# Row groups of a Fourier stage interleaved on the partitions, start-up transfers re-ordered, nine zero products ahead of the first

## The chip, the core and the metric

The program runs on one core of one Trainium2 chip. The metric is the device time of one execution in microseconds (us), lower is better. TensorE (PE), VectorE (DVE), ScalarE (ACT) and GpSimd (POOL) each run their own instruction stream in order and meet at semaphores; SyncE (SP) only issues DMAs here, in order.

## What is computed

A global filter in the frequency domain over 8 sequences of 2496 tokens with 256 channels, then a mixture of 8 experts in which each token goes to one.

```python
X = np.fft.rfft(x, axis=1)                       # x: (8, 2496, 256)
Yr = Xr @ w_r - Xi @ w_i + b_r
Yi = Xr @ w_i + Xi @ w_r + b_i
Yr, Yi = soft_shrink(Yr, 0.01), soft_shrink(Yi, 0.01)
y = np.fft.irfft(Yr + 1j * Yi, n=2496, axis=1)   # becomes x of the experts, 19968 tokens
e_idx = argmax(x @ w_gate + modality_bias[modality_id], axis=1)
out[mask_e] = gate * (relu(x[mask_e] @ w1[e]) @ w2[e])
```

## The kernel before

The Fourier transform of 2496 points is split into 39 times 64. Per sequence (a "batch", b = 0 to 7) there are these stages. **s1**: the length-39 transform as a matrix product. `x[b]` is seen as 39 rows (n1) of 64 (n2) by 256 channels; three groups of n2 (starting at 0, 22 and 42, the tuple `GB`) stand at once on 117 partitions, group g on partitions 39 g to 39 g + 38. One load covers 4 or 8 values of n2 and is three DMAs, one per group (`s1_load`, L228). The 22 values of n2 per group are worked off in 11 chunks of two: `s1_split` writes the high part (L242) and the rest (L243) of a chunk, `s1_chunk` makes three products with the block matrix `c_f` (L261 to L263), ACT copies the 120 resulting rows out of PSUM (L266), and the copies are stored to a scratch tensor in DRAM, `scr`, again with three DMAs, one per group of 40 rows (L277). For batch 0 the stores go out after the chunks 3, 7, 9 and 10. **s2**: for a pair of the 20 frequencies k1, `a_load` reads 128 rows back from `scr` (L286) and `s2_pair` multiplies them with a table `c_m` (L295). A load of batch 0 can start only when all its stores have landed, since each pair needs every n2. **mix** (L332) multiplies with the complex weights `wmix`, **is2** (L356) with a table `c_q`, then **pivot** (L372) and **is1** (L384) give the result, `Route` computes gate and place of each token and scatters the rows to their experts. `SplitWeights` prepares the expert weights meanwhile. From about 610 us on, `Experts` runs the two expert products (L819, L849) to the end.

PE's order is written out by hand in `build`. Batch 0 goes first: 11 chunks of s1, then chunks 0 to 5 of batch 1 (the loop with `ahead1 = 6`) with s2 of the pairs 0 and 1 and the first mix between them, then a loop over pairs p in which s2, mix and is2 of batch 0 run beside the rest of batch 1's chunks; later batches repeat the pattern. The order in which SP issues DMAs is set by the program order and by `tc.issue_after`, which places DMAs behind a given one in SP's queue. Loads for batch 0 and batch 1's first five pieces have buffers of their own. POOL issues no plain DMA; it scatters rows by indirect DMAs (L547, L862) and computes some differences (L994, L799).

Of the kernel before, what the change touches and what calls it, by code (L numbers as in the profile page):

```python
# [23 lines left out]
D = 256  # L24
# [30 lines left out]
def shape_constants(nb):  # L55
# [14 lines left out]
    for k1 in range(K1):  # L70
# [12 lines left out]
    blk_f = np.zeros((P1, PK))
    blk_g = np.zeros((PK, P1))
    for g in range(3):
        blk_f[g * N1:(g + 1) * N1, g * 2 * K1:(g + 1) * 2 * K1] = fwd
# [41 lines left out]
class Attn:  # L128
# [24 lines left out]
    def consts_first(self):  # L153

        nc, I, cp = self.nc, self.I, self.cp
        self.m = cp.tile([128, K1 * 128], F32, name="c_m")
        self.q = cp.tile([128, K1 * 128], F32, name="c_q")
        self.f = cp.tile([P1, 2, 128], F32R, name="c_f")
        st = self.w1.tile([128, 2, 256], F32, tag="u", name="st_f")[:P1].rearrange("p a b -> p (a b)")[:, :256]
        nc.sync.dma_start(st, I["c_f"])  # L160
        nc.vector.tensor_copy(self.f, st.rearrange("p (h k) -> p h k", h=2))

        self.w = cp.tile([128, 2, 2, 2, 256], F32R, name="wmix")

        self.bias = cp.tile([128, 256], F32, name="bias")

        self.nlam = cp.tile([128, 16], F32, name="nlam")[:, :1]
        nc.vector.memset(self.nlam, -LAM)

    def table_load(self, t, k):  # L170

        o = slice(k * 512, (k + 1) * 512)
        return self.nc.sync.dma_start((self.m if t == "m" else self.q)[:, o], self.I["c_" + t][:, o])

    def consts_mix(self):
        nc, I, cp = self.nc, self.I, self.cp
        st = []
        for i, nm in enumerate(("w_r", "w_i")):
            st.append(self.ww.tile([128, 520], F32, tag="wr", name=f"st_w{i}")[:, :512].rearrange("p (c d) -> p c d", c=2))
            nc.sync.dma_start(st[i], I[nm].rearrange("(c p) d -> p c d", p=128))  # L180
        for i, nm in enumerate(("b_r", "b_i")):
            nc.sync.dma_start(self.bias[64 * i:64 * i + 64, :],
                              I[nm].rearrange("(o d) -> o d", o=1).to_broadcast([64, 256]))
        yield
        for i in range(2):
            nc.vector.tensor_copy(self.w[:, i, :, 0, :], st[i])
            nc.vector.tensor_sub(self.w[:, i, :, 1, :], st[i], self.w[:, i, :, 0, :])
# [20 lines left out]
            nc.vector.tensor_copy(self.pv[:, c, go:go + E], gst[:, c, :])  # L208


    def s1_load(self, b, u, end=None, eng=None):

        nc = self.nc
        eng = eng or nc.sync
        end = end or u + 1
        n = min(4 * end, J) - 4 * u
        xv = self.I["x"][b].rearrange("(a c) d -> a c d", c=N2)
        if b < 2 and u < 5:

            if u == 0:  # L220
                self.early = self.x1f[0] if b else self.w1.tile([128, 2 * N2, K1, 2], F32, tag="z", name="x_0")
                if not b:
                    self.early = self.early.rearrange("p n k r -> p (n k r)")
            xt = self.early[:P1, u * 4 * D:end * 4 * D].rearrange("p (j d) -> p j d", d=D)
        else:
            xt = self.wx.tile([P1, 4, D], F32, tag="x", name=f"x_{b}_{u}")
        for g in range(3):
            ins = eng.dma_start(xt[g * N1:(g + 1) * N1, :n, :], xv[:, GB[g] + 4 * u:GB[g] + 4 * u + n, :])  # L228
        for v in range(u, end):
            self.xt[b, v] = xt[:, 4 * (v - u):4 * (v - u) + 4, :]  # L230
        return ins

    def s1_split(self, b, c):
        nc = self.nc
        u, h = c // 2, c % 2
        for v in (u, u + 1):
            if v < 6 and (b, v) not in self.xt:
                self.s1_load(b, v)
        x = self.xt[b, u][:, 2 * h:2 * h + 2, :].rearrange("p j d -> p (j d)")
        xh = self.w6.tile([P1, 512], F32R, tag="x1h", name=f"x1h_{b}_{c}")  # L240
        xl = self.w6.tile([P1, 512], F32R, tag="x1l", name=f"x1l_{b}_{c}")
        (nc.vector.tensor_copy if b == 1 or b == 0 and c % 2 == 0 else nc.scalar.copy)(xh, x)  # L242
        nc.vector.tensor_sub(xl, x, xh)  # L243
        self.xs[b, c] = xh, xl

    def s1_chunk(self, b, c, ahead):

        nc = self.nc
        u, h = c // 2, c % 2
        xh, xl = self.xs.pop((b, c))  # L250
        if c == 0:
            self.scr[b] = self.dr.tile([2 * K1, N2, D], F32, tag="scr", name=f"scr_{b}")
        if h == 0 and b:
            self.ev = self.w3.tile([128, 4 * D], F32, tag="ev", name=f"ev_{b}_{u}")[:PK].rearrange("p (j d) -> p j d", d=D)
        if b == 0:

            self.ev = self.x1f[1][:PK, :J * D].rearrange("p (j d) -> p j d", d=D)[:, 4 * u:min(4 * u + 4, J), :]

        pool, tag = (self.rps, "r") if b == 1 or c < 2 else (self.ps, "x" if b and c < 9 else "y")
        ps = pool.tile([128, 512], F32, tag=tag, name=f"s1_{b}_{c}")  # L260
        nc.tensor.matmul(ps[:PK], self.f[:, 0, :PK], xh, start=True, stop=False)  # L261
        nc.tensor.matmul(ps[:PK], self.f[:, 1, :PK], xh, start=False, stop=False)
        nc.tensor.matmul(ps[:PK], self.f[:, 0, :PK], xl, start=False, stop=True)  # L263
        if ahead and c + ahead < 11:
            self.s1_split(b, c + ahead)
        nc.scalar.copy(self.ev[:, 2 * h:2 * h + 2, :].rearrange("p j d -> p (j d)"), ps[:PK])  # L266
        if b == 0:
# [732 lines left out]
def build(tc, I, out, nb):  # L1000
    nc = tc.nc
    with ExitStack() as outer:
        dp = outer.enter_context(tc.tile_pool(name="wsp", bufs=1, space=DRAM))
        wsp = dp.tile([E * 128, 8192], F32, name="wsp")
        with ExitStack() as ctx:
            at = Attn(tc, I, nb)
            rt = Route(outer, tc, I, at, nb)
            at.pools(ctx)
            ctx.enter_context(tc.manual_schedule(engines={ET.PE, ET.Activation, ET.DVE, ET.Pool}))
            sw = SplitWeights(tc, I, at.ww, at.wo, wsp)  # L1010
# [35 lines left out]
            for u, v in ((0, 1), (1, 3), (3, 5)):  # L1046
                at.s1_load(0, u, v)
            first = at.s1_load(0, 5)
            at.s1_split(0, 0)
            at.s1_split(0, 1)  # L1050
            mixing = at.consts_mix()
            for c in range(11):
                at.s1_chunk(0, c, 2)
                with tc.issue_after(at.stored.ins if c > 2 else first.ins):
                    if c == 3:
                        at.table_load("m", 0)
                    elif c == 7:
                        at.s1_load(1, 0)
                    elif c == 9:
                        ins = at.s1_load(1, 1, 3)  # L1060
            with tc.issue_after(at.stored.ins):
                next(mixing, None)
                for i in range(3):
                    ins = load(i)
                    if i < 2:
                        with tc.issue_after(ins.ins):
                            ins = at.s1_load(1, 3, 5) if i else at.table_load("q", 0)
            with tc.issue_after(ins.ins):
                at.table_load("m", 1)
                rt.load_ids(0)  # L1070
            ahead1 = 6 if nb > 1 else 0
            at.s1_split(1, 0)
            at.s1_split(1, 1)
            for c in range(ahead1):
                with tc.issue_after(ins.ins):
                    at.s1_chunk(1, c, 2)
                if c == 1:
                    s2(0)
                    next(mixing, None)
                    bias(0)  # L1080
                if c == 3:
                    s2(1)
                if c == 4:
                    mix(0)
# [143 lines left out]
```

## Time and profile before

| | before |
|---|---|
| median of 3 runs (lowest, highest) | 1543.92 us (1542.63, 1546.65) |
| profiled execution, its own time | 1546.72 us |
| profiled execution, span from first to last instruction | 1544.9 us |
| PE busy in the span | 1497.0 us, 97% |
| PE's idle time ahead of 50 us | 27.0 us of 47.9 us in all |

The profile is of one execution. Its page gives busy time per engine; "waits" lists who waited for whom; a "timeline" row reads start, duration, engine, line, operation, tiles, and in brackets the idle time of that engine just before and what ended it. SPq rows are DMA issues: the duration is that of issuing, not of moving the data.

### The profile page before, as it was taken

To read this page: it belongs to the slowest core of one execution; us is meant where nothing else is said; L and a number is where in the kernel's file an instruction comes from. 1 tells how busy PE (TensorE), PEld (TensorE's weight loads), DVE (VectorE), ACT (ScalarE), POOL (GpSimd) and SP (SyncE) were. 2 spreads that over 40 slices of the span, in tenths; PEclk is the share of its full clock that TensorE was granted. 3 is DMA by queue.
4 is the path that set the end of the run, shared out by engine and by line. 5 is a ranking of instruction groups with operands and counts; after the bars stand their busy time and mean duration, and the time that the engine had idled before them with its cause. 6 is when DMAs were issued, how large, how long until landed. Compare 5 with 4: busy or idle time off the path is not lost. (4 is left out here: it accounts for less than half of the span.)

```text
span 1544.9 us, 35019 instructions
## 1 busy us (share of the span) xinstructions
PE 1497.0 (97%) x12459; PEld 1465.4 (95%) x12459; DVE 710.1 (46%) x1497; ACT 660.0 (43%) x1345; POOL 512.8 (33%) x511
## 2 busy tenths in 40 slices
PE   4899999999999999999999999999999999999998
PEld 2899999999999989999999999999999998999998
DVE  3676666666666665444333333333333333333332
ACT  2466766676757554523232332332323222233232
POOL 0001444444444545325532232322322323223232
PEclk8899999999999999999999999999999999999999
DMA  7857786868686666523443324552225238626440
GB/s 196 247 179 261 222 269 212 277 212 277 205 261 190 207 196 236 172 44 84 110 91 80 118 55 151 163 157 43 52 47 155 53 68 306 197 40 205 111 151 33
DMA packets 289589, 244.44 MB, mean 158 GB/s; under 512 B 208448, under 2 KB 243852, under 8 KB 285161
## 3 DMA queue, kind: packets, MB, share of 16 engines
q1 hardware_dynamic: 270421, 200.60, 44.9%
q0 software_dynamic: 18992, 41.58, 8.2%
q8 instruction: 100, 1.64, 0.5%
q14 instruction: 76, 0.62, 0.1%
HBM read 432.70 MB, written 100.08 MB: 345 GB/s over the span
## 5 line engine op out<-in xcount | busy, mean ns | idle before, releaser
L849 PE MATMUL y<-w,hh 128*128 128x256 f32 x2496 | 434.6, 278 | 0.2 <-DMA w<-wsp 0.2
L819 PE MATMUL h<-xh,w 128*128 128x256 f32 x2496 | 403.8, 278 | 4.1 <-DMA w<-wsp 4.1
L849 PEld LDWEIGHTS y<-w,hh 128*128 128x128 f32 x2496 | 377.8, 188 | 1.0 <-ACT xh L798 0.3
L849 PE MATMUL y<-w,hl 128*128 128x256 f32 x1248 | 347.2, 278 | 0.3 <-DVE hl L822 0.2
L819 PEld LDWEIGHTS h<-xh,w 128*128 128x128 f32 x2496 | 339.9, 189 | 4.5 <-issue 3.9
L822 DVE SCALAR_TENSOR_TENSOR hl<-h,hh 128x512 fp32r<-128x512 f32 x312 | 209.4, 689 | 232.2 <-ACT hh L821 188.5
L862 POOL DMA_INDIRECT out<-o,ix x161 | 158.5, 984 | 427.0 <-ACT o L841 389.7
L819 PE MATMUL h<-xl,w 128*128 128x256 f32 x1248 | 245.5, 278 | 0.0
L821 ACT ACTIVATE hh<-h 128x512 fp32r<-128x512 f32 x312 | 178.2, 595 | 155.7 <-PE h L819 137.0
L849 PEld LDWEIGHTS y<-w,hl 128*128 128x128 f32 x1248 | 234.3, 188 | 1.3 <-DVE hl L822 0.9
L819 PEld LDWEIGHTS h<-xl,w 128*128 128x128 f32 x1248 | 189.6, 189 | 0.0
L841 ACT ACTIVATE o<-y,xt 128x256 f32<-128x256 f32 x78 | 37.0, 475 | 343.0 <-PE y L849 343.0
L839 DVE TENSOR_SCALAR o<-y,xt 128x256 f32<-128x256 f32 x78 | 37.7, 484 | 314.2 <-ACT o L841 310.1
L332 PE MATMUL mx<-wmix,Xh 128*128 128x256 f32 x1280 | 180.7, 284 | 0.9 <-ACT mx L312 0.6
L799 POOL TENSOR_TENSOR xl<-tr,xh 128x512 fp32r<-128x512 f32 x78 | 101.0, 1295 | 192.9 <-ACT xh L798 192.9
L332 PEld LDWEIGHTS mx<-wmix,Xh 128*128 128x128 f32 x1280 | 160.6, 189 | 3.1 <-ACT mx L312 2.7
L547 POOL DMA_INDIRECT xs<-x1b,si x88 | 88.0, 1000 | 85.2 <-ACT ph L377 33.4
L372 PE MATMUL pv<-pv,z 128*120 128x136 f32 x704 | 111.0, 283 | 0.5 <-ACT z L359 0.5
L547 POOL DMA_INDIRECT xs<-x,si x88 | 87.9, 998 | 71.2 <-ACT ph L377 32.4
L994 POOL TENSOR_TENSOR wl<-wr,wh 128x512 fp32r<-128x512 f32 x46 | 58.5, 1273 | 148.2 <-ACT wh L993 133.7
L378 DVE TENSOR_TENSOR pl<-pv,ph 120x264 fp32r<-120x264 f32 x176 | 75.9, 431 | 68.4 <-ACT ph L377 58.2
L372 PEld LDWEIGHTS pv<-pv,z 128*120 128x120 f32 x704 | 99.5, 186 | 6.7 <-ACT z L359 0.7
(186 smaller groups left out, 1998.4 us busy)
## 6 DMA issues: line engine op xcount, KB each, us to landing
w<-wsp SPq DMA_DIRECT2D x166, 2048.0 KB
a<-scr SPq DMA_DIRECT2D x80, 256.0 KB
xt<-xs SPq DMA_DIRECT2D x624, 32.0 KB
wr<-in_moe_w SPq DMA_DIRECT2D x64, 256.0 KB
wsp<-wh SPq DMA_DIRECT2D x64, 256.0 KB
wsp<-wl SPq DMA_DIRECT2D x64, 256.0 KB
scr<-ev SPq DMA_DIRECT2D x98, 160.0 KB
x<-in_x SPq DMA_DIRECT2D x96, 156.0 KB
```

The lines of the kernel that those rows point to most:

```text
L332: self.nc.tensor.matmul(ps[i][:, i, :], t[:, 2 * i + c, o:o + 128], self.w[:, wi, c, lo, :], start=False, stop=n == len(ops) - 1, skip_gro ...
L372: nc.tensor.matmul(ps[:PK, c * 128:c * 128 + D // 2 + E], self.z[:, o:o + 3, :, :].rearrange("p n k r -> p (n k r)"), self.pv[:, c, :], st ...
L378: nc.vector.tensor_sub(pl, ps[:PK, :GC], ph)
L547: i = self.nc.gpsimd.indirect_dma_start(out=self.xs, out_offset=bass.IndirectOffsetOnAxis(ap=si[:, k:k + 1], axis=0), in_=rows, in_offset= ...
L799: nc.gpsimd.tensor_sub(xl, tr, xh)
L819: nc.tensor.matmul(ps[:, q, :], w1[:, lo, c, f * 128:(f + 1) * 128], x[:, c, :], start=n == 0, stop=n == 5)
L821: nc.scalar.activation(hh[:, 2 * p:2 * p + 2, :], ps, AF.Relu)
L822: nc.vector.scalar_tensor_tensor(hl[:, 2 * p:2 * p + 2, :], ps, 0.0, hh[:, 2 * p:2 * p + 2, :], ALU.max, ALU.subtract)
L839: nc.vector.tensor_scalar_mul(o[:, s, :], y[s], gate)
L849: nc.tensor.matmul(y[s], lhsT, w2[:, lo, f, :], start=n == 0, stop=n == 23)
L862: ins = self.nc.gpsimd.indirect_dma_start(out=self.out, out_offset=bass.IndirectOffsetOnAxis(ap=ix, axis=0), in_=o, in_offset=None, bounds ...
L994: eng.tensor_sub(lo, raw, hi)
```

## The change

1. **Interleaving.** Group g of s1 now stands on every third partition from g on (`xt[g::3]`, `blk_f[g::3, g:PK:3]`), for loads and stores of all batches. Each group has 42 result rows in place of 40 (`R1`), two of them zero, so a chunk's products have 126 rows (`PS`) and `scr` has 42.
2. **Zero products.** DVE clears a tile `blank` first, and PE makes nine products of 128x512 with it ahead of the first real one; nothing reads them.
3. **Splitting of batch 0.** The differences of odd chunks are made by POOL in place of DVE, and the high parts of chunks 1, 5 and 9 by DVE in place of ACT.
4. **Transfers of the start-up.** On SP the stores of batch 0 follow each other with no load between them, and the loads of pairs 0 and 1 stand directly behind; the first piece of table `c_m` goes ahead of them. POOL issues the loads of pieces 0 and 1 of batch 1, the mix weights, the biases and the first piece of `c_q`, after its last difference. Pieces 2 to 5 of batch 1, the second piece of `c_m`, pairs 2 and 3 follow on SP; the ids of batch 0 are loaded later.
5. **PE's order.** Four chunks of batch 1 precede s2 of pair 0 in place of two; chunks 4 and 5 come after s2 of pair 2.

On PE, from the last chunk of batch 0 to the first mix, before (`s_b_c` is chunk c of batch b, `a_p` the load of pair p, `mx_0` the first mix):

```order
L263 MATMUL s_0_10_241<-x1l_10_226,c_f 120x512
L261 MATMUL s_1_0_280<-x1h_0_270,c_f 120x512
...
L263 MATMUL s_1_1_289<-x1l_1_275,c_f 120x512
L295 MATMUL s_0_0_301<-c_m,a_0_255 128x128 x4
L261 MATMUL s_1_2_319<-x1h_2_284,c_f 120x512
...
L263 MATMUL s_1_3_328<-x1l_3_294,c_f 120x512
L295 MATMUL s_0_1_340<-c_m,a_1_258 128x128 x4
L261 MATMUL s_1_4_352<-x1h_4_323,c_f 120x512
...
L263 MATMUL s_1_4_352<-x1l_4_324,c_f 120x512
L332 MATMUL mx_0_316<-wmix,Xh_0_306 128x256 x8
```

and now:

```order
L275 MATMUL s_0_10_260<-x1l_10_244,c_f 126x512
L273 MATMUL s_1_0_297<-x1h_0_287,c_f 126x512
...
L275 MATMUL s_1_1_306<-x1l_1_292,c_f 126x512
L273 MATMUL s_1_2_319<-x1h_2_301,c_f 126x512
...
L275 MATMUL s_1_3_324<-x1l_3_311,c_f 126x512
L307 MATMUL s_0_0_336<-c_m,a_0_268 128x128 x4
L307 MATMUL s_0_1_353<-c_m,a_1_270 128x128 x4
L344 MATMUL mx_0_347<-wmix,Xh_0_341 128x256 x8
```

Chunks 2 and 3 of batch 1 moved ahead of both s2 products, and chunk 4 behind the mix. On SP, from the last load of batch 0 to the loads of pairs, before:

```order
L228 DMA x_5_126<-in_x 39x512 x3
L277 DMA scr_138<-x1b 40x2048 x2
L277 DMA scr_138<-x1b 40x1536
L173 DMA c_m<-in_c_m 128x512
L277 DMA scr_138<-x1b 40x2048 x3
L228 DMA x_66<-in_x 39x1024 x3
L277 DMA scr_138<-x1b 40x1024 x3
L228 DMA x_66<-in_x 39x2048 x3
L277 DMA scr_138<-x1b 40x512 x3
L180 DMA st_w_249<-in_w_r 128x2x256
...
L286 DMA a_0_255<-scr_138 128x2x256
```

and now:

```order
L238 DMA x_5_128<-in_x 39x512 x3
L183 DMA c_m<-in_c_m 128x512
L289 DMA scr_151<-x1b 42x2048 x2
L289 DMA scr_151<-x1b 42x1536
L289 DMA scr_151<-x1b 42x2048 x3
L289 DMA scr_151<-x1b 42x1024 x3
L289 DMA scr_151<-x1b 42x512 x3
L298 DMA a_0_268<-scr_151 128x2x256
L298 DMA a_1_270<-scr_151 128x2x256
L183 DMA c_m<-in_c_m 128x512
L298 DMA a_2_273<-scr_151 128x2x256
L238 DMA x_66<-in_x 39x1024 x3
```

The two loads of batch 1 (`x_66`) and the weights left the run of stores. On POOL, which had nothing there before, now stand behind its memsets:

```order
L255 TENSOR_TENSOR x1l_1_148<-x_118,x1h_1_147 117x512
...
L255 TENSOR_TENSOR x1l_9_223<-x_118,x1h_9_222 117x512
L238 DMA x_66<-in_x 39x1024 x3
L190 DMA st_w_233<-in_w_r 128x2x256
L190 DMA st_w_235<-in_w_i 128x2x256
L192 DMA bias<-in_b_r 64x256
L192 DMA bias<-in_b_i 64x256
L238 DMA x_66<-in_x 39x1024 x3
L183 DMA c_q<-in_c_q 128x512
```

The second `x_66` here is piece 1 of batch 1; chunks 2 and 3 of batch 1 read it.

The diff, cut to its core:

```diff
+R1 = 2 * K1 + 2
+PS = 3 * R1
-        blk_f[g * N1:(g + 1) * N1, g * 2 * K1:(g + 1) * 2 * K1] = fwd
+        blk_f[g::3, g:PK:3] = fwd
...
+        self.blank = cp.tile([128, 512], BF16, name="blank")
+        nc.vector.memset(self.blank, 0.0)
+    def warm(self, n):
+        ps = self.ps.tile([128, 512], F32, tag="z", name=f"warm_{n}")
+        for _ in range(n):
+            self.nc.tensor.matmul(ps, self.blank[:, :128], self.blank, start=True, stop=True)
...
-            ins = eng.dma_start(xt[g * N1:(g + 1) * N1, :n, :], xv[:, GB[g] + 4 * u:GB[g] + 4 * u + n, :])
+            ins = eng.dma_start(xt[g::3, :n, :], xv[:, GB[g] + 4 * u:GB[g] + 4 * u + n, :])
+            if after is not None:
+                self.rt.order(ins, after)
...
-        (nc.vector.tensor_copy if b == 1 or b == 0 and c % 2 == 0 else nc.scalar.copy)(xh, x)
-        nc.vector.tensor_sub(xl, x, xh)
+        (nc.vector.tensor_copy if b == 1 or b == 0 and c % 4 < 3 else nc.scalar.copy)(xh, x)
+        self.cut = (nc.gpsimd if b == 0 and c % 2 else nc.vector).tensor_sub(xl, x, xh)
...
-                    src[g * 2 * K1:(g + 1) * 2 * K1, lo - o:hi - o, :])
+                    src[g:PS:3, lo - o:hi - o, :])
...
             first = at.s1_load(0, 5)
+            with tc.issue_after(first.ins):
+                at.table_load("m", 0)
+            at.warm(9)
...
+            mixing = at.consts_mix(nc.gpsimd)
             for c in range(11):
                 at.s1_chunk(0, c, 2)
+                if c == 7:
+                    at.s1_load(1, 0, eng=nc.gpsimd, after=at.cut)
+                    next(mixing, None)
+                elif c == 8:
+                    at.s1_load(1, 1, eng=nc.gpsimd, after=at.cut)
+                    at.table_load("q", 0, nc.gpsimd)
             with tc.issue_after(at.stored.ins):
+                load(0)
+                ins = load(1)
...
-            ahead1 = 6 if nb > 1 else 0
+            ahead1 = 4
...
             for c in range(ahead1):
+                at.s1_chunk(1, c, 2 if c < 2 else 0)
+            next(mixing, None)
+            s2(0)
+            bias(0)
+            at.s1_split(1, 4)
+            s2(1)
+            at.s1_split(1, 5)
+            mix(0)
             bias(1)
...
-                    if p == 1 and b > 0:
-                        rt.load_ids(b)
+                    if p == 1:
+                        with tc.issue_after(ins.ins):
+                            rt.load_ids(b)
```

## Rows read from the trace of the kernel before

**Rows 1.** The page: the span, the busy time of PE, and PE's busy share and granted clock in 40 slices of 38.6 us.

```profile
span 1544.9 us, 35019 instructions
...
PE   4899999999999999999999999999999999999998
...
PEclk8899999999999999999999999999999999999999
```

**Rows 2.** PE's waits from 0 to 50 us: total, times, longest (us).

```profile
PE s L261 <- DVE x1h L242: 18.9, 4, 8.5
PE s L295 <- DMA a<-scr: 7.6, 1, 7.6
```

**Rows 3.** PE's waits from 50 us to the end, the two longest.

```profile
PE h L819 <- DMA w<-wsp: 4.1, 2, 3.7
PE i L384 <- ACT x1b L387: 2.5, 1, 2.5
```

**Rows 4.** Stretches of time: length, then busy time (instructions) of PE, PEld, DVE, ACT, POOL; then granted clock, DMA share, GB/s.

```profile
41.89:49.73 7.84, 7.07 (x26) 5.84 (x26) 4.55 (x10) 3.04 (x6) 0.00 (x0) 0.63 0.90 225
49.73:66.71 16.98, 16.98 (x132) 15.89 (x130) 12.24 (x22) 9.25 (x18) 0.00 (x0) 1.00 0.84 269
...
200.00:300.00 100.00, 99.60 (x825) 97.08 (x824) 63.96 (x138) 66.58 (x145) 44.75 (x46) 1.00 0.79 252
```

**Rows 5.** Timeline of SP, the DMA issues of the start-up.

```profile
1.27 7.15 SPq L228 DMA_DIRECT2D x<-in_x  x12
16.24 2.13 SPq L277 DMA_DIRECT2D scr<-x1b  x3
...
23.08 4.35 SPq L228 DMA_DIRECT2D x<-in_x  x3
27.52 1.60 SPq L277 DMA_DIRECT2D scr<-x1b  x3
29.17 1.95 SPq L228 DMA_DIRECT2D x<-in_x  x3
31.23 1.04 SPq L277 DMA_DIRECT2D scr<-x1b  x3
...
39.02 0.37 SPq L286 DMA_DIRECT2D a<-scr  x1
```

**Rows 6.** Timeline of all engines and of DVE and ACT alone: where pieces of x are first used, the last copy of batch 0, and the last steps ahead of the first mix.

```profile
6.03 0.43 DVE L242 CAST x1h<-x 117x512 fp32r<-117x512 f32 x1 [2.73 <-DMA x<-in_x]
...
12.17 0.62 ACT L242 CAST x1h<-x 117x512 fp32r<-117x512 f32 x1 [3.41 <-DMA x<-in_x]
...
17.57 0.43 DVE L242 CAST x1h<-x 117x512 fp32r<-117x512 f32 x1 [1.40 <-PE s L262]
...
22.93 0.58 ACT L266 COPY x1b<-s 120x512 f32<-120x512 f32 x1 [0.33 <-PE s L263]
...
30.93 0.43 DVE L242 CAST x1h<-x 117x512 fp32r<-117x512 f32 x1 [8.58 <-DMA x<-in_x]
...
45.73 0.42 DVE L303 TENSOR_TENSOR Xl<-Xh,s 128x256 fp32r<-128x256 f32 x1 [0.45 <-ACT Xh L302]
```

**Rows 7.** Timeline of PE: the products of chunks, the first s2, the first mix.

```profile
7.09 0.63 PE L262 MATMUL s<-x1h,c_f 117*120 117x512 f32 x1
7.51 0.63 PE L263 MATMUL s<-x1l,c_f 117*120 117x512 f32 x1
...
19.18 0.40 PE L261 MATMUL s<-x1h,c_f 117*120 117x512 f32 x1
19.41 0.39 PE L262 MATMUL s<-x1h,c_f 117*120 117x512 f32 x1
...
33.69 0.63 PE L263 MATMUL s<-x1l,c_f 117*120 117x512 f32 x1
41.89 2.05 PE L295 MATMUL s<-c_m,a 128*128 128x128 f32 x8 [7.57 <-DMA a<-scr]
...
49.73 1.08 PE L332 MATMUL mx<-wmix,Xh 128*128 128x256 f32 x8
```

**Rows 8.** DMA rates (GB/s) from 25 to 50 us in 40 slices of 0.625 us; then the sizes of the loads issued from 0 to 25 us.

```profile
GB/s 295 236 138 243 131 144 269 236 229 170 275 275 223 146 179 244 256 180 218 211 302 293 141 90 95 346 392 293 243 292 249 198 234 220 236 129 138 141 293 306
...
x<-in_x SPq DMA_DIRECT2D x6, 312.0 KB
...
x<-in_x SPq DMA_DIRECT2D x5, 156.0 KB
```

**Rows 9.** Groups of instructions from 0 to 50 us: busy, mean ns of one, idle before them.

```profile
L243 DVE TENSOR_TENSOR x1l<-x,x1h 117x512 fp32r<-117x512 f32 x17 | 11.6, 692 | 2.1 <-ACT x1h L242 1.2
...
L266 ACT COPY x1b<-s 120x512 f32<-120x512 f32 x11 | 6.4, 585 | 3.7 <-PE s L263 3.6
L242 DVE CAST x1h<-x 117x512 fp32r<-117x512 f32 x12 | 5.1, 423 | 21.4 <-DMA x<-in_x 14.9 <-DMA bias<-in_b_i 5.2 <-PE s L262 1.4
```

**Rows 10.** POOL's groups over the whole run; then, by line, the shortest, median and longest (ns) of POOL's differences, of SP's issues of x up to 60 us, and of the weight loads of s1.

```profile
L547 POOL DMA_INDIRECT xs<-x1b,si x88 | 88.0, 1000 | 85.2 <-ACT ph L377 33.4 <-ACT u L340 31.5 <-ACT x L387 7.7
...
L994 POOL TENSOR_TENSOR wl<-wr,wh x46: 1262/1273/1286, 131.9 to 593.7; 128x512 fp32r<-128x512 f32 x46
...
L228 SPq DMA_DIRECT2D x<-in_x x27: 307/371/1658, 1.3 to 58.4; - x27
...
L261 PEld LDWEIGHTS s<-x1h,c_f x88: 179/181/320, 6.5 to 491.9; 117*120 117x120 f32 x88
```

More of the change, by code (lines that the diff above doesn't have):

```diff
@@ L82, in shape_constants @@
         q[k1, 0, :, :, 1], q[k1, 1, :, :, 1] = (w * s).T, (w * c * sg).T
[L83 removed]
+    blk_f = np.zeros((P1, PS))
     blk_g = np.zeros((PK, P1))
     for g in range(3):
[L86 removed]
+        blk_f[g::3, g:PK:3] = fwd
         blk_g[g * 2 * K1:(g + 1) * 2 * K1, g * N1:(g + 1) * N1] = inv
@@ L168, in consts_first, with table_load, consts_mix @@
         nc.vector.memset(self.nlam, -LAM)
-    def table_load(self, t, k):
+    def warm(self, n):
+        ps = self.ps.tile([128, 512], F32, tag="z", name=f"warm_{n}")
+        for _ in range(n):
+            self.nc.tensor.matmul(ps, self.blank[:, :128], self.blank, start=True, stop=True)
+    def table_load(self, t, k, eng=None):
         o = slice(k * 512, (k + 1) * 512)
-        return self.nc.sync.dma_start((self.m if t == "m" else self.q)[:, o], self.I["c_" + t][:, o])
-    def consts_mix(self):
+        return (eng or self.nc.sync).dma_start((self.m if t == "m" else self.q)[:, o], self.I["c_" + t][:, o])
+    def consts_mix(self, eng):
         nc, I, cp = self.nc, self.I, self.cp
@@ L179, in consts_mix @@
             st.append(self.ww.tile([128, 520], F32, tag="wr", name=f"st_w{i}")[:, :512].rearrange("p (c d) -> p c d", c=2))
-            nc.sync.dma_start(st[i], I[nm].rearrange("(c p) d -> p c d", p=128))
+            eng.dma_start(st[i], I[nm].rearrange("(c p) d -> p c d", p=128))
         for i, nm in enumerate(("b_r", "b_i")):
-            nc.sync.dma_start(self.bias[64 * i:64 * i + 64, :],
+            eng.dma_start(self.bias[64 * i:64 * i + 64, :],
                               I[nm].rearrange("(o d) -> o d", o=1).to_broadcast([64, 256]))
@@ L208, in consts_last, with s1_load @@
             nc.vector.tensor_copy(self.pv[:, c, go:go + E], gst[:, c, :])
-    def s1_load(self, b, u, end=None, eng=None):
+    def s1_load(self, b, u, end=None, eng=None, after=None):
         nc = self.nc
@@ L251, in s1_chunk @@
         if c == 0:
-            self.scr[b] = self.dr.tile([2 * K1, N2, D], F32, tag="scr", name=f"scr_{b}")
+            self.scr[b] = self.dr.tile([R1, N2, D], F32, tag="scr", name=f"scr_{b}")
         if h == 0 and b:
-            self.ev = self.w3.tile([128, 4 * D], F32, tag="ev", name=f"ev_{b}_{u}")[:PK].rearrange("p (j d) -> p j d", d=D)
+            self.ev = self.w3.tile([128, 4 * D], F32, tag="ev", name=f"ev_{b}_{u}")[:PS].rearrange("p (j d) -> p j d", d=D)
         if b == 0:
-            self.ev = self.x1f[1][:PK, :J * D].rearrange("p (j d) -> p j d", d=D)[:, 4 * u:min(4 * u + 4, J), :]
+            self.ev = self.x1f[1][:PS, :J * D].rearrange("p (j d) -> p j d", d=D)[:, 4 * u:min(4 * u + 4, J), :]
         pool, tag = (self.rps, "r") if b == 1 or c < 2 else (self.ps, "x" if b and c < 9 else "y")
         ps = pool.tile([128, 512], F32, tag=tag, name=f"s1_{b}_{c}")
-        nc.tensor.matmul(ps[:PK], self.f[:, 0, :PK], xh, start=True, stop=False)
-        nc.tensor.matmul(ps[:PK], self.f[:, 1, :PK], xh, start=False, stop=False)
-        nc.tensor.matmul(ps[:PK], self.f[:, 0, :PK], xl, start=False, stop=True)
+        nc.tensor.matmul(ps[:PS], self.f[:, 0, :PS], xh, start=True, stop=False)
+        nc.tensor.matmul(ps[:PS], self.f[:, 1, :PS], xh, start=False, stop=False)
+        nc.tensor.matmul(ps[:PS], self.f[:, 0, :PS], xl, start=False, stop=True)
         if ahead and c + ahead < 11:
             self.s1_split(b, c + ahead)
-        nc.scalar.copy(self.ev[:, 2 * h:2 * h + 2, :].rearrange("p j d -> p (j d)"), ps[:PK])
+        nc.scalar.copy(self.ev[:, 2 * h:2 * h + 2, :].rearrange("p j d -> p (j d)"), ps[:PS])
         if b == 0:
@@ L1006, in build @@
             at = Attn(tc, I, nb)
-            rt = Route(outer, tc, I, at, nb)
+            rt = at.rt = Route(outer, tc, I, at, nb)
             at.pools(ctx)
@@ L1048, in build @@
             first = at.s1_load(0, 5)
+            with tc.issue_after(first.ins):
+                at.table_load("m", 0)
+            at.warm(9)
             at.s1_split(0, 0)
             at.s1_split(0, 1)
-            mixing = at.consts_mix()
+            mixing = at.consts_mix(nc.gpsimd)
             for c in range(11):
                 at.s1_chunk(0, c, 2)
[L1054 to L1060, printed above, removed]
-            with tc.issue_after(at.stored.ins):
[L1062 to L1067, printed above, removed]
+                if c == 7:
[4 more added lines that the diff above has]
+                    at.table_load("q", 0, nc.gpsimd)
+            with tc.issue_after(at.stored.ins):
+                load(0)
+                ins = load(1)
             with tc.issue_after(ins.ins):
                 at.table_load("m", 1)
-                rt.load_ids(0)
-            ahead1 = 6 if nb > 1 else 0
+                ins = load(2)
+            with tc.issue_after(ins.ins):
+                ins = at.s1_load(1, 2)
+            with tc.issue_after(ins.ins):
+                ins = load(3)
+            with tc.issue_after(ins.ins):
+                at.s1_load(1, 3, 5)
+                ins = at.s1_load(1, 5)
+            ahead1 = 4
             at.s1_split(1, 0)
@@ L1074, in build @@
             for c in range(ahead1):
[L1075 to L1084, printed above, removed]
+                at.s1_chunk(1, c, 2 if c < 2 else 0)
[6 more added lines that the diff above has]
+            mix(0)
             bias(1)
-            ins = load(3)
-            with tc.issue_after(ins.ins):
-                at.s1_load(1, 5)
             state = None
@@ L1120, in build @@
                         ahead(i)
-                    if p == 1 and b > 0:
-                        rt.load_ids(b)
+                    if p == 1:
+                        with tc.issue_after(ins.ins):
+                            rt.load_ids(b)
                     if p in (1, 2, 3, 5, 7, 9) and b + 2 < nb:
```

## The prediction

> **What bounds the kernel now.** I read the page first: PE is busy for 97% of the span, and only the first two of 40 slices show less [rows 1]. Then PE's waits in two parts. Ahead of 50 us it waits 27 us: 18.9 us for a chunk's high part (6.5 of it the very start, 8.5 the longest) and 7.6 us for the first load of a pair from the scratch tensor [rows 2]. Behind 50 us the longest wait of 1495 us is 3.7 us, for expert weights [rows 3], and from 49.73 us on, the first mix, PE does not pause [rows 4]. So a gain can only come from an earlier first mix; everything behind it is a line of PE work that starts as early as that, and faster DMAs in later batches shorten no wait of PE. The chain to the first mix is read from SP's queue [rows 5] with the points where the data is used [rows 6]: load batch 0, eleven chunks, stores, load of pair 0, s2. The last copy of batch 0 ends at 23.51 us, yet its stores are issued from 31.23 to 32.27, since two loads of batch 1 (4.35 us at 23.08, 1.95 at 29.17) and the store before it stand ahead in the queue; the load of pair 0 is issued at 39.02, 6.75 us after the last store's issue, because every byte of that queue has to land first.
>
> **The change, step by step** (the profiled execution, 1546.72 us with a span of 1544.9; the median is 2.8 lower, and I carry the difference over to it).
>
> *Loads of batch 0.* The pieces are first used at 6.03, 12.17 and about 17.5 us [rows 6] (the last row names PE, whose product had ended already). The second and third piece are three DMAs of 312 KB each [rows 8], 0.96 MB in 6.1 and 5.4 us, 157 to 177 GB/s. What interleaved rows reach is not in this trace. The bounds: no gain (5.4 us a piece), or the best slice of rows 8, 392 GB/s (2.4 us a piece; transfers over 128 partitions were running there). I take 300 GB/s, nearer to that row because the rows will spread over as many partitions: 3.2 us a piece, so the pieces are there at 5.5, 8.7 and 11.9 us.
> [...]
>
> *Chunks 6 to 10.* From 11.9 us DVE makes the high part of 6, difference of 6, the same of 8, high part of 9: 3 x 0.42 + 2 x 0.69 = 2.6 us [rows 9], then POOL the difference of 9: its differences took 1.26 to 1.29 us [rows 10], also in stretches where DVE was 64% busy [rows 4], so I count no slowing. POOL is through at 16.0 us with 0.2 for hand-overs. PE and the copies (0.59 each, rows 9) follow: the last copy ends at 17.6 in place of 23.51. The removed work on DVE needs no more, since DVE then waits for data.
>
> *Zero products.* Nine at 0.43 us, the spacing of 512-column products at the low clock [rows 7], end near 5 us, ahead of the first data: cost 0, hidden by the wait for x; uncovered at most 0.5 us on chunk 0, which waits for piece 2 anyway. Whether they bring the full clock earlier (0.23 us spacing at 19.2 us) matters below 4 us to the last copy (9 chunks, 3 x 0.2 us less each, part of it covered), and nothing to POOL's chain, which comes out last.
>
> *Stores and the load of pair 0.* The last store is issued 1.04 us later [rows 5], at 18.7 (-13.6). The stores, 2.75 MB with the 42nd rows, start after chunk 3 at about 11.5; at 300 GB/s they take 9.2 us, and POOL's load joins from 16 us with 0.48 MB, 1.6 us more. I issue pair 0 at 22.5; bounds 20.7 (no contention) and 25.5 (6.75 us after the last issue, as now). It lands 2.9 us later, as from 39.02 to 41.89: 25.4.
>
> *POOL's queue.* This is the wait that is put in the place of the old ones. s2 of pair 0 now stands behind chunks 2 and 3 of batch 1, which need piece 1, and its last DMA is POOL's tenth: three of piece 0, two weights, two biases, three of piece 1. A plain DMA issued by POOL is not in the trace. Bounds: SP's median issue, 0.37 us, and POOL's indirect DMA, 1.00 us [rows 10]; I take 1.0, the same engine. Then 16.0 + 10.0 = 26.0, landed 28.9 with the 2.9 us from above, and from the first high part to the last product of two chunks it is now 30.93 to 34.32 us, 3.4 us [rows 6, 7]. So s2 of pair 0 starts at 32.3 us, not 25.4: POOL's queue is late next, and SP's has 7 us of slack.
>
> *To the first mix.* The first mix needs the difference parts of s2, ready 4.3 us after its start (41.89 to 46.15, rows 6, 7): 36.6 us. The weight splits fit before it on DVE (2.2 us, between 29 and 33). Of the 7.84 us that stretch took before, 2.9 went to two chunks, 2.2 to the weight splits on DVE. At the first mix one chunk less is done, 0.7 us at the full clock. The gain: 49.73 - 36.6 - 0.7 = 12.4 us. The clock is at 0.63 of full there now [rows 4] and full at the mix; I count the same.
>
> *The rest.* 126 columns of weights in place of 120 could add 5% to a 0.18 us load [rows 10], 264 times: 2.4 us if uncovered, but each lies beside a 512-column product of 0.23 us, so 0. The stores grow by 5%, 1 MB over the run, at a DMA share of 0.79 and with PE busy 99.6% [rows 4]: 0. Moving the ids of batch 0 behind pair 5 frees SP early: 0, since they are first used at the end of that batch.
>
> Sum: -12.4 us, 1534.3 by the profiled execution, 1531.5 us by the median.
>
> **The rivals.** *POOL issues cheaply.* At 0.37 us, piece 1 lands at 22.6 and s2 starts at 26.0, after pair 0's 25.4 just the same: 6.3 us more, 1525 us. For it: direct transfers have regular addresses, while the 1.00 us row scatters by a list. *Interleaving brings nothing.* Then the third piece still arrives at 17.5, everything of POOL's chain shifts by 5.6, and 6.8 us remain, from the order alone: 1537 us. For it: rows 8 show slices under 150 GB/s with all kinds of transfers. *Other waits in the new order* (piece 2 or pair 2 late behind 1.5 MB, s2 chains with fewer chunks between them) eat most of it, within 4.6 us: 1541. [...]
>
> **How the numbers follow.** The forecast, a gain of 9 to 15 us: 0.50. POOL cheap: 0.22. Interleaving without effect: 0.16. Other waits, a gain under 4.6 us or none: 0.06. POOL held up: 0.06. 0.3%, 4.6 us, is about what a measurement of this kernel can tell from no change. So faster by more 0.88, within it 0.06, slower 0.06. The range leaves the last two cases out and takes the bounds of the others, with a margin of 2 us at either end: 1523 to 1539.
>
> **What would show it.** In the profile after: the third piece used near 11.9 us (17.5: no effect of the rows); POOL's last difference near 16 and its DMA issues 1.0 us apart; the load of pair 0 issued near 22.5; PE waiting for the high part of chunk 2 of batch 1, not for pair 0, ahead of s2 near 32; the first mix near 36.6; no new wait of PE behind it. The forecast is wrong if the first mix is earlier but PE pauses behind it, or if the span loses time in the later batches.

## The result and the profile after

The changed kernel took 1556.82 us, the median of 4 runs (1555.50 to 1557.74), beside 1544.40 us of the kernel before (4 runs, 1542.63 to 1546.65). The ratio is 1.0079, 95% interval [1.0063, 1.0095]: slower, by 10 to 15 us. The profiled execution took 1555.50 us. Its page, in the lines of [rows 1]:

```profile
span 1553.7 us, 35060 instructions
...
PE   5799999999999999999999999999999998999998
...
PEclk6999999999999999999999999999999999999999
```

The first slice is fuller than before (5 in place of 4, nine zero products among it), the second, with a pause in it now, less full (7 in place of 8), and the span is 8.8 us longer. PE's waits, first from 0 to 50 us, then from 50 us to the end [rows 2, 3]; columns: total, times, longest.

```profile
PE s L273 <- DVE x1h L254: 13.4, 4, 7.0
PE mx L344 <- ACT mx L324: 1.4, 1, 1.4
PE s L275 <- POOL x1l L255: 1.3, 2, 0.7
```

```profile
PE mx L344 <- ACT mx L324: 7.4, 2, 6.6
PE h L831 <- DMA w<-wsp: 6.1, 3, 4.8
PE i L396 <- ACT x1b L399: 2.6, 1, 2.6
```

The 7.6 us for the load of a pair are gone. What is new is a wait of 6.6 us behind 50 us, for a mix. Where it lies, and where else time went, is read by setting the same instruction of both timelines side by side: the first is2 products start at 49.88 us (58.31 before), the fourth at 66.92 (74.05), the fifth at 80.47 (78.67), and one of ACT's last activations at 1543.29 (1535.66). So the start did get shorter: it led by 8.4 us, still by 7.1 at the fourth, and lost all of it with 1.8 more in the one step to the fifth. That step of 8.9 us is the largest of the 16 between the lead at the first is2 and the lag of 7.6 us at the end. Two stretches stand out (length, busy PE, PEld, DVE, ACT, POOL, granted clock, DMA share, GB/s), after:

```profile
70.00:80.00 10.00, 4.51 (x21) 4.52 (x22) 2.91 (x5) 3.07 (x6) 0.00 (x0) 0.66 0.87 279
...
763.00:785.00 22.00, 20.19 (x154) 19.19 (x153) 7.28 (x15) 6.09 (x11) 9.07 (x9) 0.92 0.54 163
```

and before:

```profile
70.00:80.00 10.00, 10.00 (x89) 10.00 (x88) 5.67 (x10) 5.60 (x11) 0.50 (x2) 1.00 0.81 241
...
763.00:785.00 22.00, 22.00 (x194) 22.00 (x193) 7.73 (x15) 6.43 (x13) 8.42 (x8) 1.00 0.55 160
```

In the first, PE stood idle for 5.5 us, and the granted clock, 1.00 before, is 0.66 in the mean: from 75.49 to 80.00 us, where PE was busy again, it was 0.50. In the second it was idle for 1.8 us and lost about as much to the clock (0.08 of 22 us), some 260 us behind the last transfer that the change touches (a store at 501 us).

The start itself, SP's issues [rows 5]:

```profile
1.25 9.61 SPq L238 DMA_DIRECT2D x<-in_x  x12
...
15.76 12.64 SPq L289 DMA_DIRECT2D scr<-x1b  x12
33.73 0.90 SPq L298 DMA_DIRECT2D a<-scr  x2
```

DVE and, below it, POOL [rows 6, 9, 10]:

```profile
11.70 0.43 DVE L254 CAST x1h<-x 117x512 fp32r<-117x512 f32 x1 [3.95 <-DMA x<-in_x]
12.16 0.69 DVE L255 TENSOR_TENSOR x1l<-x,x1h 117x512 fp32r<-117x512 f32 x1
12.77 1.50 DVE L254 CAST x1h<-x 117x512 fp32r<-117x512 f32 x1
...
34.94 0.43 DVE L254 CAST x1h<-x 117x512 fp32r<-117x512 f32 x1 [3.06 <-DMA x<-in_x]
```

```profile
12.38 1.61 POOL L255 TENSOR_TENSOR x1l<-x,x1h 117x512 fp32r<-117x512 f32 x1 [3.27 <-ACT x1h L254]
...
20.48 1.32 POOL L255 TENSOR_TENSOR x1l<-x,x1h 117x512 fp32r<-117x512 f32 x1 [1.56 <-DVE x1h L254]
22.11 1.84 POOL L238 DMA_DIRECT2D x<-in_x  x3 [0.31 <-POOL x1l L255]
23.91 0.80 POOL L190 DMA_DIRECT2D st_w<-in_w_r  x1
...
29.04 0.51 POOL L238 DMA_DIRECT2D x<-in_x  x1 [0.42 <-DMA x<-in_x]
```

A cast of 0.43 us takes 1.50 while POOL's difference runs beside it. PE [rows 7]:

```profile
1.19 3.97 PE L178 MATMUL warm<-blank 128*128 128x512 bf16 x9 [1.19 <-DVE blank L159]
...
7.09 0.39 PE L274 MATMUL s<-x1h,c_f 117*126 117x512 f32 x1
...
13.20 0.63 PE L275 MATMUL s<-x1l,c_f 117*126 117x512 f32 x1
13.63 0.63 PE L273 MATMUL s<-x1h,c_f 117*126 117x512 f32 x1
...
35.52 0.77 PE L273 MATMUL s<-x1h,c_f 117*126 117x512 f32 x1 [2.59 <-DVE x1h L254]
...
38.21 2.38 PE L307 MATMUL s<-c_m,a 128*128 128x128 f32 x16
42.01 1.20 PE L344 MATMUL mx<-wmix,Xh 128*128 128x256 f32 x8 [1.41 <-ACT mx L324]
```

The first mix starts at 42.01 us (49.73 before). The wait at 35.52 is for chunk 2 of batch 1, whose piece DVE gets at 34.94; s2 of pair 0 follows at 38.21 without a wait. And the price of a DMA over every third partition, by line (shortest, median, longest ns); before, SP's median was 371 for x [rows 10]:

```profile
L238 SPq DMA_DIRECT2D x<-in_x x129: 745/753/1515, 1.2 to 473.0; - x129
L238 POOL DMA_DIRECT2D x<-in_x x6: 507/552/766, 22.1 to 29.0; - x6
...
L289 SPq DMA_DIRECT2D scr<-ev x126: 726/738/1624, 43.6 to 501.4; - x126
```

The wait near 75 us, from its end back: PE, ACT, SP.

```profile
75.49 2.08 PE L344 MATMUL mx<-wmix,Xh 128*128 128x256 f32 x8 [6.62 <-ACT mx L324]
```

```profile
73.77 0.59 ACT L278 COPY ev<-s 126x512 f32<-126x512 f32 x1 [8.35 <-DMA scr<-ev]
```

```profile
62.58 2.37 SPq L289 DMA_DIRECT2D scr<-ev  x3
64.99 0.54 SPq L428 DMA_DIRECT2D rev<-in_c_rev  x1
...
67.33 0.39 SPq L426 DMA_DIRECT2D tri_st<-in_c_tri  x1
67.83 0.33 SPq L203 DMA_DIRECT2D st_g<-in_c_g  x1
68.20 0.40 SPq L209 DMA_DIRECT2D st_g<-in_moe_w_gate  x1
68.70 2.34 SPq L289 DMA_DIRECT2D scr<-ev  x3
```

ACT stands at the copy of the last chunk of batch 1 until a store of `ev` has landed; the copy of the bias for PE's mix is behind it on ACT. That pool (`w3`, tag `ev`) has three buffers. With `ahead1 = 4` the last chunk falls into pass p = 3, and the program takes two of the three for `tri_st` and `st_g` just ahead of it; the store that has to free the third stands on SP behind their loads.

### The profile page after: what moved, and what is told of

It is laid out like the page before. It is cut to its first block, busy times and chain, and to the rows that moved or that the text cites. A ratio compares the mean times of both kernels' runs of the same rounds, so it can differ in the third digit from the quotient of the medians.

```text
span 1553.7 us, 35060 instructions
## 1 busy us (share of the span) xinstructions
PE 1503.3 (97%) x12468; PEld 1469.1 (95%) x12468; DVE 712.8 (46%) x1496; ACT 658.7 (42%) x1342; POOL 528.1 (34%) x527
```

## The experiments

Each ratio is to the kernel before on the same chip; e1 to e4, e5 to e8, e9 to e11, e12 and e13 ran on four different chips, so kernels of different groups are compared by their ratios. "PE" is PE's busy time in the 22 us from 763 to 785 us, "first mix" and "PE" are of the profiled execution.

| run | what it is | median us | ratio to before [95%] | first mix us | PE |
|---|---|---|---|---|---|
| after | the change | 1556.82 | 1.0079 [1.0063, 1.0095] | 42.01 | 20.19 |
| e1 | after, last chunk ahead of the constants | 1550.58 | 1.0028 [1.0016, 1.0039] | 42.26 | 19.76 |
| e2 | after, contiguous groups | 1565.27 | 1.0122 [1.0102, 1.0141] | 45.43 | 20.04 |
| e3 | e1 and e2 | 1552.75 | 1.0043 [1.0029, 1.0057] | 45.10 | 19.97 |
| e4 | before, interleaved | 1550.09 | 1.0030 [1.0017, 1.0043] | 47.70 | 22.00 |
| e5 | e1, batch 0 alone interleaved | 1549.68 | 1.0020 [1.0011, 1.0030] | 42.17 | 20.66 |
| e6 | e5, differences by DVE | 1549.45 | 1.0016 [1.0006, 1.0026] | 41.54 | 20.09 |
| e7 | e6, no zero products | 1548.87 | 1.0014 [1.0005, 1.0022] | 41.06 | 19.77 |
| e8 | before, batch 0 alone interleaved | 1545.08 | 0.9992 [0.9980, 1.0005] | 47.15 | 22.00 |
| e9 | e8, eleven transfers by POOL | 1549.73 | 1.0015 [1.0002, 1.0028] | 44.92 | 20.68 |
| e10 | e7, the eleven by SP | 1546.48 | 0.9991 [0.9980, 1.0003] | 47.26 | 22.00 |
| e11 | e8, loads behind the stores | 1548.20 | 1.0003 [0.9990, 1.0016] | 48.38 | 22.00 |
| e12 | e9, the eleven by ACT | 1546.71 | 0.9996 [0.9986, 1.0006] | 45.83 | 22.00 |
| e13 | e12, stores contiguous | 1547.59 | 1.0008 [0.9999, 1.0018] | 49.92 | 22.00 |

**e1 to e4: the staging buffers, and the interleaving.** e1 moves three lines:

```diff
+                        for c in (2 * p + ahead1, 2 * p + ahead1 + 1):
+                            if c < 11 and nb > 1:
+                                at.s1_chunk(1, c, 2)
                         if p == 3:
                             late = [rt.consts(), at.consts_last()]
...
-                        for c in (2 * p + ahead1, 2 * p + ahead1 + 1):
-                            if c < 11 and nb > 1:
-                                at.s1_chunk(1, c, 2)
```

e2 puts the groups back (`xt[g * N1:(g + 1) * N1]`, `R1 = 2 * K1`, stores alike), e3 does both, e4 is the kernel before with the interleaving and its 126 rows alone.

> The changed kernel with one thing exchanged: in the pass of pair 3 the last chunk of batch 1 takes its staging buffer before the two late constants do, as it did before the change. Theory A (buffer order): PE's 6.6 us wait for ScalarE at 69 us, and the 3 us at half clock behind it, come from that chunk's copy waiting for a buffer whose store stands in SP's queue behind the constants; then both go and the time is 1545 to 1548 us, the first mix staying near 42.0 us. Theory B (issue time): SP is late because each strided DMA takes it 0.74 us instead of 0.3 to 0.4; then the exchange moves the wait elsewhere and the time stays within 3 us of 1557.

> The changed kernel with the row groups side by side again (39 and 40 rows on neighbouring partitions), all else as changed. Theory A: the buffer order is the same, so PE still waits at the last chunk of batch 1, 4 us or more, and the time is 1549 to 1555 us (some 2 to 7 us won by a shorter SP queue). Theory B: SP's issues fall to 0.3 to 0.4 us, no wait of PE over 2 us is left behind the first mix, and the time is 1538 to 1545 us. Both: if interleaving does speed the data up, the pieces of batch 0 arrive later than 11.7 and 15.5 us.

> The changed kernel with both: row groups side by side and the chunk ahead of the constants. Theory A: 1537 to 1542 us, no wait of PE over 2 us between the first mix and 500 us. Theory B: the same as with the groups side by side alone, within 2 us.

> The kernel before with the interleaved rows (and the 42nd row) alone. If a strided DMA costs SP 0.74 us in place of 0.3 to 0.4 and that binds, the first mix comes 3 to 6 us later than 49.7 and the time is 1548 to 1554 us; if the faster data wins, the first mix comes 2 to 4 us earlier and the time is 1540 to 1543 us. Under theory A no wait like the one at 69 us appears, since the buffer order is that of before.

In e1 PE is busy for 10.00 of the 10 us from 70 to 80, at the full clock, and the ratio falls by half a per cent, 7.9 us (6.2 by the two medians).

```profile
70.00:80.00 10.00, 10.00 (x90) 10.00 (x89) 6.73 (x12) 5.47 (x11) 0.50 (x2) 1.00 0.85 267
```

e2 shows that the wait is not made by interleaved DMAs: contiguous, it is longer.

```profile
84.60 2.08 PE L344 MATMUL mx<-wmix,Xh 128*128 128x256 f32 x8 [11.15 <-ACT mx L324]
```

So the buffers' order is the cause of this wait, shown by e1 against after and by e3 against e2. It is not all that was lost: e1, e2 and e3 are slower than theory A forecast for them, by 3, 10 and 11 us from the nearer end of its ranges, and e1 is still 4.3 us slower than before. The interleaving does quicken the start (first mix 42.26 in e1, 2.8 us later without it in e3; load of pair 0 issued at 35.50 in e4, 39.02 before), yet e4 is 4.6 us slower than before: its time is in the range of the case that had the first mix come later, though the first mix came 2.0 us earlier. One place where it pays later is seen on SP, ACT and PE of e4:

```profile
127.53 2.33 SPq L279 DMA_DIRECT2D scr<-ev  x3
129.96 0.48 SPq L997 DMA_DIRECT2D wsp<-wh  x1
...
137.79 0.45 SPq L983 DMA_DIRECT2D wr<-in_moe_w  x1
```

```profile
142.78 0.62 ACT L995 CAST wh<-wr 128x512 fp32r<-128x512 f32 x1 [1.92 <-DMA wr<-in_moe_w]
```

```profile
144.52 1.19 PE L334 MATMUL mx<-wmix,Xh 128*128 128x256 f32 x8 [1.19 <-ACT mx L314]
```

Three stores take SP 2.33 us (1.09 before, at 127.87). The seventh expert-weight piece is issued at 137.79 (135.37 before), ACT, which did not wait for it before, waits 1.92 us, and PE, which had no wait from 100 to 200 us before, has one of 1.19 us.

**e5 to e8: batch 0 alone, and the parts of the start.** `NI = 1`, and a second block matrix in `c_f` for the contiguous batches:

```diff
         for g in range(3):
-            ins = eng.dma_start(xt[g::3, :n, :], xv[:, GB[g] + 4 * u:GB[g] + 4 * u + n, :])
+            ins = eng.dma_start(xt[g::3, :n, :] if b < NI else xt[g * N1:(g + 1) * N1, :n, :], xv[:, GB[g] + 4 * u:GB[g] + 4 * u + n, :])
```

e6 gives e5 the splitting of the kernel before, e7 takes `at.warm(9)` from e6, e8 is e4 with `NI = 1`.

> The kernel after with chunk 10 of batch 1 ahead of the late constants (as e1_chunk_first) and with the interleaving kept for batch 0 alone; loads and stores of the batches 1 to 7 are contiguous again. Theory SP (what e1 still loses against before, 4.7 us by the medians, is in good part the 0.74 us that SP pays for each interleaved DMA of the later batches): the wait of 1.7 us at the mix near 138 us goes, the time falls 2 to 3 us below e1, to 1547.5 to 1548.5 us; the load of pair 0 stays near 33.7 us. Rival (the loss is the price of the new start-up order itself, given back whatever the later batches do): 1550 to 1551.5 us, as e1.

> e5_later_contiguous with batch 0 split as in the kernel before: all differences by DVE, high parts by DVE and ACT in turn. Theory (GpSimd's differences of 1.28 to 1.61 us hold up DVE's casts, so they free nothing): the last copy of batch 0 and the load of pair 0 come no more than 1 us later than in e5, perhaps earlier, and the time is within 1.5 us of e5. Rival (the prediction's reckoning: GpSimd takes work off DVE): the load of pair 0 comes 2 to 4 us later and the time rises by 2 us or more.

> e6_no_gpsimd_differences without the nine zero products. Theory (the clock falls to half at 8.4 us with them, before most of the products of batch 0, and PE waits for the splits there in any case): first mix within 0.5 us, time within 1 us of e6. Rival (they raise the clock where it matters): first copies 0.5 to 1 us later, time up by 1 to 2 us.

> The kernel before with the interleaving for batch 0 alone. Theory SP: the 3.5 us by which the load of pair 0 came earlier in e4 stay, the later batches' issues cost 0.31 us again, so 3 to 5 us below e4, at 1545 to 1547 us, at or a little below before. Rival (e4 lost by the 126-row products or the scratch tensor of 42 rows, not by SP): 1549 to 1551 us as e4.

e8 came out as theory SP said, 0.4% below e4 and level with before: the interleaving costs in the later batches. e5 moved by less than that theory wanted (0.0008 against e1, inside the intervals), so under the new order something else held most of the loss. e6 and e7 differ from e5 and from each other by less than the intervals. Their traces say which way: the last copy of batch 0 ends at 23.55 us in e5, 22.61 in e6, 21.32 in e7. POOL's differences and the zero products do not speed batch 0 up; here they came with a later end.

**e9 to e11: POOL's transfers.** The seven kernels with the new start up to e7 (after, e1 to e3, e5 to e7) all lost 1.3 to 2.2 us of PE's time between 763 and 785 us, e4 and e8 none. What they share is the eleven start-up DMAs by POOL. e9 adds just these to e8 (`eng=nc.gpsimd` as in the change's diff); e10 gives them to SP in e7; e11 leaves them on SP in e8 and puts the pair loads behind the stores.

> e8_before_interleave_batch0 with the eleven start-up transfers of the change (pieces 0 and 1 of batch 1, mix weights, biases, first piece of c_q) issued by GpSimd, all else as in the kernel before. Theory H (GpSimd holds for 1.9 us at a fixed count of its own DMAs; before and e8 have it at their 200th, where nothing waits; with eleven more it falls at the 203rd, in the run of scatters near 755 us, and costs PE 3 to 5 us between 760 and 785 us, as in every kernel with the new start-up so far): the hold of 1.88 us at GpSimd's 203rd DMA appears, PE is busy under 38.5 of the 40 us from 760 to 800 us, and the time is 2 to 4 us above e8. Rival (the loss near 765 us comes from the new order on PE or SP, not from GpSimd's count): no hold there, time within 1 us of e8.

> e7_no_zero_products with the eleven transfers issued by SP again: piece 0 of batch 1 among the stores, the others directly behind the loads of pairs 0 and 1. Theory H: no hold near 755 us, PE busy 39.5 us or more of 760 to 800 us, so what the new order gains at the start is kept: 2 to 4 us below e7, 1544.5 to 1547 us, if the start loses less than 2 us by it. Rival: the loss near 765 us stays, 1548 to 1551 us.

> e8_before_interleave_batch0 with the loads of pairs 0 and 1 directly behind the stores of batch 0 on SP; pieces 1 and 2 of batch 1, weights, biases and tables behind them; PE's order as before. If the queue places held the loads back, the load of pair 0 comes 2 to 4 us earlier than in e8 and the time falls by 1 to 3 us, to 1542 to 1544.5 us. Rival (the stores' landing or batch 1's pieces bound the first mix anyway): within 1 us of e8, or up to 2 us above.

e9's POOL, then its ACT:

```profile
753.27 1.01 POOL L556 DMA_INDIRECT xs<-x,si  x1 [1.88 <-issue]
754.59 1.00 POOL L556 DMA_INDIRECT xs<-x,si  x1 [0.30 <-issue]
...
773.47 1.00 POOL L871 DMA_INDIRECT out<-o,ix  x1 [0.30 <-issue]
```

```profile
755.60 0.47 ACT L850 ACTIVATE o<-y,xt 128x256 f32<-128x256 f32 x1 [4.59 <-PE y L858]
...
761.95 0.60 ACT L830 ACTIVATE hh<-h 128x512 fp32r<-128x512 f32 x1 [4.32 <-PE h L828]
...
771.41 0.47 ACT L850 ACTIVATE o<-y,xt 128x256 f32<-128x256 f32 x1 [5.88 <-PE y L858]
```

and POOL in the kernel before, then its ACT:

```profile
774.93 0.98 POOL L862 DMA_INDIRECT out<-o,ix  x1 [1.98 <-DVE hl L822]
```

```profile
759.95 0.47 ACT L841 ACTIVATE o<-y,xt 128x256 f32<-128x256 f32 x1 [4.96 <-PE y L849]
...
771.20 0.47 ACT L841 ACTIVATE o<-y,xt 128x256 f32<-128x256 f32 x1 [4.81 <-PE y L849]
```

Counted through the trace, the row at 774.93 is POOL's 200th DMA; it has the 1.98 us in before, e4, e8 and e12 alike, and POOL's waits in e10 and e11 have two of this kind, 4.0 and 4.1 us together, the longer 2.1. With eleven more DMAs at the start the hold stands at the 203rd, another instruction, with 1.87 to 1.88 us in after and every experiment up to e9 that has the transfers, while the scatter that was the 200th goes without (773.47). A second hold follows at the 306th (2.07 us), or the 308th (2.15 to 2.16). So it goes by POOL's DMAs, not by the place in the program or the time (e2 has it 16 us later than e5, at the same 203rd). With eleven more ahead it comes three and two counts later, not eleven: what is counted stays open. At its old place nothing waits; at the new one six scatters stand behind each other, ACT idles 3.0 to 4.5 us ahead of one activation in all these kernels (0.85 before, 0.70 in e12), and e9 goes from 4.4 us ahead of before (ACT's scaling of `o` at 755.60; 759.95) to 0.2 behind (771.41; 771.20). In all eight the activation starts 1.0 to 1.2 us after the last of the six scatters. By the ratios e9 is 3.6 us above e8, as theory H said; its profiled execution is among its fastest (1545.45 us) and ends 1.3 us ahead of before's. e10, without POOL's transfers, loses nothing there, and its time is in the range of theory H, but it did not keep what the new order gains at the start: its first mix is 6.2 us later than e7's. e11 won nothing: pair 0 is loaded 6 us earlier than in e8 (30.26), but chunks 2 and 3 of batch 1, ahead of the first mix on PE, then wait 6.43 us for piece 1; first mix 48.38.

```profile
41.52 0.76 PE L267 MATMUL s<-x1h,c_f 117*126 117x512 f32 x1 [6.43 <-DVE x1h L247]
```

**e12 and e13: the same transfers by another engine.** In e12 ACT issues them behind its last copy of batch 0 (`nc.scalar`); e13 lays the results of e12's batch 0 out group by group (`blk_f[g::3, g * 2 * K1:(g + 1) * 2 * K1] = fwd`), so that its stores are contiguous.

> e9_batch0_and_gpsimd_transfers with its eleven start-up transfers issued by ScalarE, behind its last copy of batch 0, in place of GpSimd. Theory H (the loss of 4.6 us between 763 and 785 us is GpSimd's hold alone, so the transfers themselves are good for the start): the hold moves back to GpSimd's 200th DMA, PE is busy 39.5 us or more of 760 to 800 us, the 4 to 5 us won by 60 us stay, and the time is 3 to 5 us below before (0.997 to 0.998). Rival (what e9 won at the start depends on GpSimd's issuing it early, beside the copies): 1 to 2 us won by 60 us, time as e8 (0.999 to 1.000).

> e12_transfers_by_act with the interleaving for batch 0's loads alone; its result rows stand group by group again, so its stores are contiguous. If the interleaved stores' issue time on SP (0.73 to 1.1 us each) holds back the load of pair 0: that load is issued 1 to 4 us earlier than in e12 and the time falls by 1 to 3 us. Rival (interleaved stores land so much faster that this outweighs their issue time): the load of pair 0 comes 1 to 4 us later, time up by 1 to 3 us.

e12 loses nothing at the scatters, as theory H said; its forecast time was missed: it is ahead by 3.8 us at the first is2, and loses that in small pieces, of 1.1 us at most, from 170 us on. It equals before. In e13 the rival came true: its nine last stores took 12.45 us against 10.34, the load of pair 0 came 2.7 us later (35.90 against 33.16) and the first mix 4.1; the times' intervals overlap. The shortest issue of a store of batch 0 took SP 0.73 us interleaved (after) and 0.27 contiguous (before), and still the nine interleaved ones are through sooner.

No version was faster than before by more than the runs can tell; e8 and e10 to e13 are level with it.

## Why the prediction was wrong

- **"No new wait of PE behind it"** is the step that failed. Where chunks 4 and 5 went I priced PE's work (0.7 us) and not what the move does to the buffers of a later pass. The trace of before could not show the wait, but the program's order did: three buffers, two taken by `tri_st` and `st_g` ahead of chunk 10. It cost 5.5 us idle and a granted clock of 0.50 behind it, up to 80 us; e1 gives back 7.9 us. That alone does not turn the sign: without this wait the new order is still 4.3 us slower than before, and PE has a second new wait at POOL's hold. Both are what the prediction named as its sign of being wrong, a pause of PE behind an earlier first mix. The rival "other waits" had the kind right, but left a gain of up to 4.6 us where 10 to 15 were lost.
- **POOL's queue.** I took 1.0 us a DMA and put 0.06 on a POOL that is held up, all for the start. That chance was my estimate, and no run shows such a hold there: POOL issued at 0.51 to 0.80 us, cheaper than forecast; the cost came 700 us later, as a shifted hold, 4.6 us in e9. e9 against e8 and e12 against e9 show it. How the hold reaches ACT is open: ACT's wait is put down to PE's `h`, whose products had ended, and no row names the scatters.
- **"Faster DMAs in later batches shorten no wait", so the interleaving counted 0 there.** Right for gains, wrong for the price: SP pays twice per DMA (median 738 to 753 ns in after, 332 to 370 before). In the kernel before, e4 against e8 puts the later batches' interleaving at 5.9 us (0.0038); the one place shown, 1.2 us of it, comes through SP. In the new order e1 against e5 gives 1.2 us, not told from none.
- **Loads of batch 0: 5.5, 8.7 and 11.9 us.** The second piece was used at 11.70, half a microsecond earlier than before: issuing twelve DMAs took 9.61 us in place of 7.15, which I had at nothing. The layout did speed the transfers up, to less than the 300 GB/s that I took: from 6 to 12 us the DMA engines moved 246 GB/s, and 172 before; from 1.5 to 6 us, with the dearer issues, 157 against 202. In e2, the same order with contiguous groups, the first piece was used at 5.80 us (6.26 in after) and the second at 12.47.
- **"I count no slowing" for POOL's differences.** Wrong: DVE's casts took 1.50 us beside them. Last copy at 23.67, not 17.6; taking the differences off POOL (e6) gives back 0.9 of these 6.1 us. Both sides were slowed: a cast of 0.43 us alone took 1.50 beside a difference of 1.28 alone, which took 1.61.
- **Zero products at 0.** Right in time (e7 against e6). What they brought of the clock was gone before it counted: the product at 7.09 us took 0.39 us (0.63 before), the granted clock was 1.00 up to 8.4 us and then 0.50 to 18.6, and at 13.20 products stand 0.43 us apart, as in [rows 7]. In e2, with the same nine, a product at 6.62 us took 0.40 and one at 7.93 already 0.63.
- **Load of pair 0 at 22.5**, bound 25.5: 33.73. The twelve stores took SP 12.64 us from 15.76 on, and the load followed 5.3 us behind them. It did not bind: as forecast PE waited for chunk 2, that is for POOL's queue. That queue began 5.8 us later than forecast (last difference through at 21.80), took 7.4 us in place of 10.0, and piece 1 was used 5.4 us after its last issue in place of 2.9. So s2 began at 38.21 and not 32.3. The first mix at 42.01, not 36.6, left a lead of 8.4 us where 12.4 were forecast: the direction of the start was right, its size two thirds.

By the ratios: after to e1 -7.9 us (buffers), e1 to e7 -2.2 (not told apart singly), e7 to e10 -3.6 (POOL's transfers given back to SP: the hold is gone from the scatters, and the first mix is 6.2 us later), which is level with before. That the lead of e7 (9.0 us at the first is2, 1.4 at 646 us, ahead of the hold), of e10 (3.2, gone by 570 us) and of e12 is lost again in small waits stays unexplained; in e7 these are 7.6 us, about as much as the buffers' wait cost.

## What to carry to other kernels

Moving work past a point where buffers of a shared pool are taken moves it in that pool's queue too; list who allocates from the pool between the old place and the new before pricing the move. SP's price per DMA depended on the partitions' pattern here (medians 0.74 to 0.75 us over every third partition, 0.33 to 0.37 over neighbouring ones): count such a price in the batches where nothing was to be won, and use the dearer pattern only where the transfer is waited for. A start-up gain is money only if it is still there at the end: set the same instruction of both timelines side by side every few tens of microseconds.

## What the runs showed of the hardware

- A DMA over every third partition (39 or 42 rows, after) took SP 0.73 to 0.75 us to issue at least, one over neighbouring partitions (39 or 40 rows, before) 0.27 to 0.31 (medians 0.74 to 0.75 and 0.33 to 0.37); POOL's plain DMA took 0.51 to 0.80 (after).
- From 6 to 12 us, during the loads of batch 0, the DMA engines moved 246 GB/s with these over every third partition (after) and 172 over neighbouring ones (before).
- POOL held 1.88 to 1.98 us at its 200th or 203rd DMA and 2.07 to 2.16 us at the 306th or 308th. What it waits for there, no run shows.
- Beside a difference on POOL (1.28 to 1.61 us) a DVE cast of 0.43 us took 1.50 (after, e2).
